# A transformer block on one core: where the output-projection weights live, when a second FFN group may open, and how the last chunk is normalized

## The chip, the cores and the metric

The kernel runs on one core of one Trainium2 chip. The metric is the device time of one execution in microseconds. Seven runs of the kernel before the change are shown, and one execution was profiled. PE is the matmul engine (TensorE), PEld its weight loads, DVE the vector engine, ACT the scalar engine, POOL GpSimd, and SP the engine that issues every DMA here.

## The reference

One pre-norm transformer block over 2048 tokens of width 1024, in bf16, with 32 heads of 32 and an FFN of width 3584:

```python
def _A_ref(x, wqkv, wo):            # attention, H = 32, Dh = 32
    ...
    scores = jnp.einsum("bhqd,bhkd->bhqk", q, k) * scale
    p = _softmax(scores, axis=-1)
    o = jnp.einsum("bhqk,bhkd->bhqd", p, v)
    return (lambda x, *d: x.transpose(*d))(o, 0, 2, 1, 3).reshape(B, S, D) @ wo

def _B_ref(x, w1, b1, w2, b2):      # FFN
    h = jnp.einsum("bsd,df->bsf", x, w1) + b1
    h = _gelu(h)                    # tanh form
    return jnp.einsum("bsf,fd->bsd", h, w2) + b2

h = x + _A_ref(_layernorm(x, axis=-1), A_wqkv, A_wo)
h2 = h + _B_ref(_layernorm(h, axis=-1), B_w1, B_b1, B_w2, B_b2)
```

## The kernel before

The tokens are cut into eight chunks of 256. Heads are handled in eight groups g of four. For each chunk c the kernel runs `attention(c)`: for each g, eight rounds over 256 keys. A round is eight score matmuls (L680), two exponentials of 128x1024 on ACT (L688), a sum of pairs PS on DVE (L693), eight matmuls with V (L698) and four with ones for the denominator (L717). At the end of a group DVE scales the result into `OT` (L726 to L734).

Beside attention runs the background work of the chunks before it. Its matmuls are all recorded by the helper `mm` (L493 in the form of four column tiles, L496 in the full form that is used after the last attention matmul). For chunk c it is, in this order: `wo(c)`, the output projection, four groups (j, t) of 8 matmuls 128x512, j being the half of the 1024 output columns and t the tile of 128 tokens; DVE adds the rows of x (L762) into `hch`; `ln2(c)`, the normalization of both tiles into `xb` (bn_stats L541, bn_aggr L543, small steps on POOL L546 to L552, normalization L555) and a transposition into `hnT` (by DMA, in the last chunk by PE and ACT, L561 and L564); `ffn1(c)`, 14 blocks of 16 matmuls with a GELU on DVE and ACT (L798 or L794, L801, L802, L804, L806) into `gT`; and `ffn2(c)`, four groups (j, t) of 29 matmuls, the first of which adds the bias, with a last step L826 and the store. ffn2(c) is interleaved with ffn1(c+1) by `PLAN`: one group, 4 blocks, one group, 5 blocks, one group, 5 blocks, one group.

Weights come in blocks of 512 KB through two rings: `w1r` with three slots and `w2r` with seven. ffn1 takes one block of w1r per block of work; ffn2 takes seven blocks of w2r for each j. wo takes four blocks: of w1r in chunks 0, 1 and 7, of w2r in chunks 2 to 6.

The order on each engine is written ahead of time by a planner in the program (`Graph.schedule`): it plays all tasks with assumed durations, and each engine's instructions are then issued in the order that it found, with semaphore waits between engines. On DVE, ACT, POOL and SP it takes the ready task with the smallest `prio`, then the oldest. On PE it takes scores first, then attention's other matmuls, then background matmuls, by the age of their group (`pick_pe`). A background group needs one of the free PSUM banks, of which attention leaves two to be shared between its own accumulator and the background. A group may open when all that it reads is done or nearly so, except what stands in its `soft` set, when each task of its `gate` has been placed, and when its loads can be issued; after attention's last matmul the oldest group may open at once. A buffer (`Buf`) is what dependencies are counted on: a task that reads a buffer waits for its writers.

After attention(7) comes the tail: half of ffn2(6), wo(7), ln2(7), the other half of ffn2(6), ffn1(7), ffn2(7). It has wider rings, `R2`, made from the memory of K and V (`slots`, names wk and wv), which is free by then.

Of the kernel before, what the change touches and what calls it, by code (L numbers as in the profile page):

```python
# [12 lines left out]
P = 128  # L13
# [299 lines left out]
def build_kernel(nc, A_x, A_wqkv, A_wo, B_w1, B_b1, B_w2, B_b2, out):  # L313
# [80 lines left out]
    RB, B_RB = sb(top, "RB", [P, NFI, 8], F32, NFI)  # L394
    pt_hi = top.cur
    NOT = 2
    OT, B_OT_ = sb(top, "OT", [P, NOT, G, 256], BF, NOT * G)
    B_OT = [B_OT_[G * s:G * s + G] for s in range(NOT)]
    NXR = 8
# [28 lines left out]
    R1 = Set()  # L428
    NW1, NW2 = 3, 7
    w1r, B_w1r = sb(ffn, "w1r", [P, NW1, 2048], BF, NW1)  # L430
    hch, B_hch_ = sb(ffn, "hch", [P, 2, 2, D], BF, 4)
    B_hch = [B_hch_[:2], B_hch_[2:]]
    x_lo = ffn.cur
    R1.x = Ring(ring(ffn, "a_x", 2, 512, BF))
    xb2 = ring(Area(x_lo), "xb2", 1, D, BF)[0]
    hnT, B_hnT = sb(ffn, "hnT", [P, 2, DC, P], BF, 2)
    R1.sq = Ring(ring(ffn, "a_sq", 2, 512, BF))
    th_lo = ffn.cur
# [94 lines left out]
    def layer_norm(tiles, prio):  # L533
        n = len(tiles)
        while cnt["ln"] % NLN + n > NLN:
            cnt["ln"] += 1
        i = cnt["ln"] % NLN
        cnt["ln"] += n
        for k, (x_ap, B_x, o_ap, B_o) in enumerate(tiles):
            for c in range(2):  # L540
                dve(lambda v, c=c, k=k, x_ap=x_ap: v.bn_stats(st_l[:, i + k, 6 * c:6 * c + 6], x_ap[:, 512 * c:512 * c + 512]),  # L541
                    0.68, reads=[B_x], writes=[B_stl[i + k]], prio=prio)
            dve(lambda v, k=k: v.bn_aggr(mv_l[:, i + k, :], st_l[:, i + k, :]), 0.2,  # L543
                reads=[B_stl[i + k]], writes=[B_mv[i + k]], prio=prio)
        sl = slice(i, i + n)
        pool(lambda g: g.tensor_copy(mvb[:, sl, :], mv_l[:, sl, :]), 0.25, reads=B_mv[sl], writes=B_mvb[sl], prio=prio)  # L546
        dve(lambda v: v.tensor_copy(mvr[:, sl, :], mvb[:, sl, 0:1]), 0.2, reads=B_mvb[sl], writes=B_mvr[sl], prio=prio)
        pool(lambda g: g.tensor_scalar(tb[:, sl, :], mvb[:, sl, 1:2], EPS_BF, None, ALU.add), 0.25,
             reads=B_mvb[sl], writes=B_tb[sl], prio=prio)
        pool(lambda g: g.tensor_tensor(denb[:, sl, 0], tb[:, sl, 0], cexp[:, 0:n], ALU.pow), 0.42 + 0.157 * n,  # L550
             reads=B_tb[sl] + [B_cexp], writes=B_denb[sl], prio=prio)
        pool(lambda g: g.tensor_tensor(rden[:, sl, 0], denb[:, sl, 0], cexp[:, 8:8 + n], ALU.pow), 0.4 + 0.157 * n,  # L552
             reads=B_denb[sl] + [B_cexp], writes=B_rden[sl], prio=prio)
        for k, (x_ap, B_x, o_ap, B_o) in enumerate(tiles):
            dve(lambda e, k=k, x_ap=x_ap, o_ap=o_ap: e.tensor_scalar(  # L555
                o_ap, x_ap, mvr[:, i + k, :], rden[:, i + k, :], ALU.subtract, ALU.mult), 0.58,
                reads=[B_x, B_mvr[i + k], B_rden[i + k]], writes=[B_o], prio=prio)

    def transposes(g, src_ap, B_src, dst_ap, B_dst, evac):
        for dc in range(DC):  # L560
# [20 lines left out]
            P * DC * (c1 - c0) * 2, writes=B_W[blk][c0 // P:c1 // P], prio=prio, after=after)  # L581

    def x_slot(tt):
        return xrb[:, tt % NXR, :], B_xrb[tt % NXR]

    def x_tile(tt, prio):
        ap, b = x_slot(tt)
        return dma(ap, x2[tt * P:(tt + 1) * P, :], P * D * 2, writes=[b], prio=prio)

    def ln_tiles(tts, prio):  # L590
        layer_norm([x_slot(tt) + (xb[:, tt % NXB, :], B_xb[tt % NXB]) for tt in tts], prio)
# [157 lines left out]
    def rows(ap, c, t, j):  # L749
        return ap[256 * c + P * t:256 * c + P * t + P, 512 * j:512 * j + 512]  # L750

    def wo(R, c, ring_):
        for j in range(2):
            ws = [w2block(ring_, A_wo[512 * q:512 * q + 512, 512 * j:512 * j + 512]) for q in range(2)]
            for t in range(2):
                x3, bx = R.x.next()
                dma(x3, rows(x2, c, t, j), P * 1024, writes=[bx], prio=1, after=lx)
                grp = group(f"wo{c}.{j}{t}")
                for g in range(G):
                    w, bw, _ = ws[g // 4]  # L760
                    mm(grp, OT[:, c % NOT, g, t * P:t * P + P], w[:, g % 4, :], g == 0, g == G - 1, [B_OT[c % NOT][g], bw])
                dve(lambda v, t=t, j=j, x3=x3, grp=grp: v.tensor_tensor(  # L762
                    hch[:, c % 2, t, 512 * j:512 * j + 512], psum[:, grp.bank, :], x3, ALU.add),
                    c_dve_ps(512), reads=[grp.buf, bx], writes=[B_hch[c % 2][t]], prio=-2)

    def ln2(c, evac):
        o, bo = xb2
        for t in range(2):
            layer_norm([(hch[:, c % 2, t, :], B_hch[c % 2][t], o, bo)], 0)
            if evac == "dma":  # L770
                dma_t(hnT[:, t, :, :], o, [bo], [B_hnT[t]], prio=-1)
            else:
                transposes(group(f"t{c}.{t}"), o, bo, hnT[:, t, :, :], B_hnT[t], evac)

    soft = {}

    def ffn1(R, c, blks, tail=False):
        for blk in blks:
            w, bw = wblock(R, B_w1[:, 256 * blk:256 * blk + 256])
            grp = group(f"f1.{c}.{blk}")  # L780
            for f in range(2):
                for dc in range(DC):
                    mm(grp, w[:, dc, f * P:f * P + P], hnT[:, :, dc, :], dc == 0, dc == DC - 1, [bw] + B_hnT,
                       cols=(256 * f, 256 * f + 256))
            (sq, b_sq), (th, b_th) = R.sq.next(), R.th.next()
            fc = 2 * blk
            xh = gT[:, c % 2, fc:fc + 2, :]
            b_xh = B_gT[c % 2][fc:fc + 2]

            def v2(ap):  # L790
                return ap.rearrange("p (f n) -> p f n", f=2)
            if tail:
                for f in range(2):
                    act(lambda a, xh=xh, f=f, fc=fc, grp=grp: a.activation(  # L794
                        xh[:, f, :], psum[:, grp.bank, 256 * f:256 * f + 256], ACT.Identity,
                        bias=b1f[:, fc + f:fc + f + 1], scale=1.0), 256, reads=[grp.buf, B_b1f], writes=[b_xh[f]], ap_bias=True)
            else:
                dve(lambda v, xh=xh, fc=fc, grp=grp: v.tensor_tensor(  # L798
                    xh, v2(psum[:, grp.bank, :]), b1f[:, fc:fc + 2].unsqueeze(2).broadcast_to((P, 2, 256)), ALU.add),
                    c_dve_ps(512), reads=[grp.buf, B_b1f], writes=b_xh, prio=-2)  # L800
            dve(lambda v, sq=sq, xh=xh: v.tensor_tensor(v2(sq), xh, xh, ALU.mult), c_dve(512, 2), reads=b_xh, writes=[b_sq], prio=1)  # L801
            dve(lambda v, sq=sq, xh=xh: v.scalar_tensor_tensor(v2(sq), v2(sq), C2, xh, ALU.add, ALU.mult), c_dve(512),  # L802
                reads=[b_sq] + b_xh, writes=[b_sq], prio=1)
            act(lambda a, th=th, sq=sq: a.activation(th, sq, ACT.Tanh, bias=0.0, scale=K2 / 2), 512,  # L804
                reads=[b_sq], writes=[b_th], prio=-1, kind="tanh")
            t = dve(lambda v, th=th, xh=xh: v.scalar_tensor_tensor(xh, v2(th), 1.0, xh, ALU.add, ALU.mult),  # L806
                    c_dve(512), reads=[b_th] + b_xh, writes=b_xh, prio=1)
            soft.setdefault(c, set()).add(t)
# [3 lines left out]
    def ffn2(R, c, j, t, tail=False):  # L812
# [3 lines left out]
        grp = group(f"f2.{c}.{j}{t}")  # L816
        grp.soft = {d for _, _, d in ws}
        grp.dmas = [d for _, _, d in ws]
        if tail:
            pass  # L820
        mm(grp, two_row[:, :], b2t[:, 512 * j:512 * j + 512], True, False, [B_two, B_b2t])
        for fc in range(FC):
            w, bw, _ = ws[fc // 4]
# [1 line left out]
        o, bo = R.os.next()  # L825
        dve(lambda v, j=j, t=t, o=o, grp=grp: v.scalar_tensor_tensor(  # L826
            o, psum[:, grp.bank, :], 0.5, hch[:, c % 2, t, 512 * j:512 * j + 512], ALU.mult, ALU.add),
            c_dve_ps(512), reads=[grp.buf, B_hch[c % 2][t]], writes=[bo], prio=-2)
        dma(rows(out2, c, t, j), o, P * 1024, reads=[bo], prio=0)

    def mixed(R, c1, c2, plan):
# [84 lines left out]
        attend(g, 0)  # L916
        attend(g, 1)

    wo(R1, 0, R1.w1)
    ln2(0, "dma")  # L920
    for k in range(4):
        late_q(2, k)
    for k in range(4):
# [8 lines left out]
            if g % 2 == 1 and c + 2 < NC:  # L932
                load_q(c + 2, g // 2)

    F2 = [(0, 0), (0, 1), (1, 0), (1, 1)]
    PLAN = [F2[0], 4, F2[1], 5, F2[2], 5, F2[3]]
    ffn1(R1, 0, range(FC // 2))
    for c in range(2, NC):
        wo(R1, c - 1, R1.w1 if c == 2 else R1.w2)
        ln2(c - 1, "dma")  # L940
        mixed(R1, c - 1, c - 2, PLAN)
        attention(c)
    L = NC - 1
    TA = 2
    tail = Area(pt_lo, pt_hi)
    R2 = Set()
    R2.sq = Ring(ring(tail, "b_sq", 4, 512, BF))
    R2.th = Ring(ring(tail, "b_th", 4, 512, F32))
    R2.os = Ring(ring(tail, "b_os", 2, 512, BF))
    slots = []  # L950
    for k in range(7):
        for lo, nm in ((kt_lo, "wk"), (v_lo, "wv")):
            slots += ring(Area(lo + 4096 * k), f"{nm}{k}", 1, 2048, BF)
    for jt in F2[:TA]:
        ffn2(R1, L - 1, *jt)
    wo(R1, L, R1.w1)
    ln2(L, "act")
    for jt in F2[TA:]:
        ffn2(R1, L - 1, *jt)
    k = R1.w1.k % NW1  # L960
    R2.w1 = Ring(slots[:11] + R1.w1.slots[k:] + R1.w1.slots[:k])
    R2.w2 = Ring(slots[11:] + R1.w2.slots)
    ffn1(R2, L, range(FC // 2), True)
    for jt in F2:
        ffn2(R2, L, *jt, True)
# [161 lines left out]
```

## Time and profile before

| | |
|---|---|
| median of 7 runs | 1144.76 us (1141.82 to 1148.82) |
| the profiled execution | 1144.76 us, span 1143.0 us |
| busy PE / ACT / DVE | 1070.1 / 1037.8 / 823.5 us |
| L688, the exponentials | 1024 instructions, 967.0 us busy |
| L493, ffn1's matmuls | 6272 instructions, 221.2 us busy |
| loads w2r<-wo / w1r<-wo | 20 / 12 issues of 512 KB |
| mean granted TensorE clock | 0.990 |

A row of the profile gives a line of the kernel, the engine, the operation, the tile written and the tiles read, the number of instructions, and the busy time. The four column tiles of one background matmul count as four instructions, and overlap. A number in square brackets in a timeline is the time that the engine stood idle before this row, with what released it. The time of one execution is 1.8 us longer than the profile's span, which runs from the first instruction to the last.

### The profile page before, as it was taken

The numbers are of one execution on the slowest core, as the hardware profiler recorded it, in microseconds if no ns is written. First come the engines' busy times: TensorE is split into PE (matmuls) and PEld (weight loads), VectorE is DVE, ScalarE is ACT, GpSimd is POOL, SyncE is SP. The second block draws the span as 40 slices with busy tenths as digits, with TensorE's granted clock in tenths as the row PEclk, the third lists the DMA queues.
The fourth block names the chain that finished last, engine by engine and source line by source line (L and its number), as shares of the span: only waits on it lengthen the run. The fifth ranks groups of instructions, "written<-read, shape, count | busy, mean of one in ns | idle before, by whom it ended". The sixth has DMA issues, their size and how long they took to land.

```text
span 1143.0 us, 53683 instructions
## 1 busy us (share of the span) xinstructions
PE 1070.1 (94%) x24933; PEld 608.8 (53%) x24939; DVE 823.5 (72%) x1552; ACT 1037.8 (91%) x1185; POOL 43.8 (4%) x108
## 2 busy tenths in 40 slices
PE   8979999999999989999999999999998989899998
PEld 6636464655445535654654555455545634555484
DVE  7345666666768977886897878777877866777572
ACT  4869999999999999999999999999999999999460
POOL 3200000000100010001000100100010001000000
PEclk9989999999999989999999999999999989999999
DMA  8860100001435536476637574764657456868742
GB/s 208 179 152 5 47 4 3 3 22 49 118 99 162 154 100 208 130 220 186 199 110 234 152 213 132 209 205 131 208 154 232 116 175 180 270 187 261 241 134 92
DMA packets 265137, 168.09 MB, mean 147 GB/s; under 512 B 56017, under 2 KB 262865, under 8 KB 264914
## 3 DMA queue, kind: packets, MB, share of 16 engines
q1 hardware_dynamic: 264914, 164.67, 49.3%
q8 instruction: 195, 3.19, 1.1%
q14 instruction: 28, 0.23, 0.1%
HBM read 151.00 MB, written 6.29 MB: 138 GB/s over the span
## 4 chain that ended last, share of the span: by engine, by line
PE 53%; ACT 34%; DVE 5%; DMA 3%; SPq 2%; issue 2%; POOL 1%; DVEq 0%; POOLq 0%
ACT PT L688 32%; PE ps L493 30%; PE ps L680 8%; PE ps L496 5%; PE ps L698 5%; PE ps L717 3%; ACT a_th L804 2%; SPq L514 2%; DVE gT L798 1%; PE ps L850 1%; DMA hnT<-xb 1%; DVE PS L693 1%; DMA q_scratch<-stg 1%; DMA b1b<-in_B_b_dram 1%; DVE gT L806 1%
## 5 line engine op out<-in xcount | busy, mean ns | idle before, releaser
L688 ACT ACTIVATE PT<-ps 128x1024 bf16<-128x1024 f32 x1024 | 967.0, 1050 | 35.8 <-PE ps L680 32.7
L693 DVE TENSOR_TENSOR PS<-PT 128x1024 bf16<-128x1024 bf16 x496 | 329.1, 683 | 87.7 <-ACT PT L688 49.8
L493 PE MATMUL ps<-hnT,w1r 128*32 128x256 bf16 x6272 | 221.2, 274 | 17.5 <-issue 6.8
L680 PE MATMUL ps<-QT,KT 32*128 32x256 bf16 x4096 | 206.1, 275 | 16.5 <-ACT PT L688 12.7
L698 PE MATMUL ps<-PT,V 128*32 128x256 bf16 x4096 | 188.6, 275 | 14.0 <-ACT PT L688 10.1
L493 PE MATMUL ps<-w2r,gT 128*32 128x512 bf16 x2936 | 196.8, 382 | 0.6 <-issue 0.6
L493 PEld LDWEIGHTS ps<-hnT,w1r 128*32 128x32 bf16 x6272 | 155.4, 96 | 60.3 <-issue 44.8
L680 PEld LDWEIGHTS ps<-QT,KT 32*128 32x128 bf16 x4096 | 61.1, 92 | 170.9 <-ACT PT L688 124.0
L717 PE MATMUL ps<-PS,ones 128*32 128x256 bf16 x1984 | 143.5, 277 | 2.7 <-DVE PS L693 1.3
L493 PE MATMUL ps<-xnT,Wall 128*32 128x512 bf16 (+1 forms) x2144 | 129.9, 357 | 7.6 <-DVE QT L574 6.5
L698 PEld LDWEIGHTS ps<-PT,V 128*32 128x32 bf16 x4096 | 99.1, 96 | 65.5 <-ACT PT L688 30.9
L493 PEld LDWEIGHTS ps<-w2r,gT 128*32 128x32 bf16 x2936 | 69.8, 96 | 66.4 <-issue 23.7
L798 DVE TENSOR_TENSOR gT<-ps,b1f 128x512 bf16<-128x512 f32 x98 | 67.3, 687 | 34.3 <-PE ps L493 33.2
L717 PEld LDWEIGHTS ps<-PS,ones 128*32 128x32 bf16 x1984 | 53.0, 96 | 43.5 <-DVE PS L693 28.4
L493 PEld LDWEIGHTS ps<-xnT,Wall 128*32 128x32 bf16 x2144 | 51.0, 97 | 46.0 <-issue 14.5
L806 DVE SCALAR_TENSOR_TENSOR gT<-a_th,gT 128x512 bf16<-128x512 f32 x98 | 67.2, 685 | 11.5 <-ACT a_th L804 11.2
L802 DVE SCALAR_TENSOR_TENSOR a_sq<-a_sq,gT 128x512 bf16<-128x512 bf16 x98 | 66.7, 687 | 1.4
L804 ACT ACTIVATE a_th<-a_sq 128x512 f32<-128x512 bf16 x98 | 64.2, 656 | 2.3 <-DMA q_scratch<-stg 1.5
L493 PE MATMUL ps<-Wall,xnT 128*32 128x256 bf16 x1536 | 51.3, 273 | 1.6 <-DVE KT L574 1.0
L493 PE MATMUL ps<-w2r,OT 128*32 128x512 bf16 x640 | 46.1, 391 | 1.1 <-DVE hch L762 0.5
L546 POOL CAST mvb<-mv 128x2 bf16<-128x2 f32 (+1 forms) x24 | 4.9, 203 | 1036.2 <-DVE mv L543 1031.8
L726 DVE STREAM_TRANSPOSE DT<-ps 128x256 f32<-128x256 f32 x64 | 28.6, 447 | 21.0 <-PE ps L717 20.8
(76 smaller groups left out, 687.5 us busy)
## 6 DMA issues: line engine op xcount, KB each, us to landing
w2r<-in_B_w_dram SPq DMA_DIRECT2D x106, 512.0 KB, 6.2
w1r<-in_B_w_dram SPq DMA_DIRECT2D x101, 512.0 KB, 4.2
w2r<-in_A_wo_dram SPq DMA_DIRECT2D x20, 512.0 KB, 5.6
w1r<-in_A_wo_dram SPq DMA_DIRECT2D x12, 512.0 KB, 3.8
wv<-in_B_w_dram SPq DMA_DIRECT2D x9, 512.0 KB, 5.3
xrb<-in_A_x_dram SPq DMA_DIRECT2D x16, 256.0 KB, 3.9
Wall<-in_A_wqkv_dram SPq DMA_DIRECT2D x16, 256.0 KB, 5.1
a_x<-in_A_x_dram SPq DMA_DIRECT2D x32, 128.0 KB, 2.7
```

The source lines that it names most:

```text
L493: fns.append(lambda p, j=j: p.matmul(dst(32 * j, 32 * j + 32), lhsT[:, 32 * j:32 * j + 32], rhs, start=start, stop=stop, tile_position=(0, ...
L496: t.alt = [lambda p: p.matmul(dst(0, P), lhsT, rhs, start=start, stop=stop, skip_group_check=True)]
L680: fns.append(lambda p, i=i, hh=hh, r0=r0: p.matmul(psum[:, 2 * us[hh // 2] + hh % 2, 256 * i:256 * i + 256], KT[r0:r0 + 32, g, 256 * r + P ...
L688: act(lambda a, u=u, q=q: a.activation(PT[:, s, 2 * q:2 * q + 2, :], psum[:, 2 * u:2 * u + 2, :], ACT.Exp, bias=0.0, scale=SCALE), 1024, r ...
L693: dve(lambda v: v.tensor_tensor(PS[:, z, :, :], PT[:, s, :, 0:256], PT[:, s, :, 256:512], ALU.add), c_dve(1024, 2), reads=B_PT[s], writes= ...
L698: fns.append(lambda p, i=i, hh=hh: p.matmul(psum[32 * hh:32 * hh + 32, self.bank, 0:256], V[:, g, 2 * r + i, 32 * hh:32 * hh + 32], PT[:, ...
L717: fns.append(lambda p, i=i, hh=hh, src=src: p.matmul(psum[32 * hh:32 * hh + 32, self.bank, 256:512], ones32[:, :], src[:, hh, :], start=False,
L726: dve(lambda v: v.transpose(DT[:, f, :], psum[:, self.bank, 256:512]), c_dve_ps(256), reads=[self.buf], writes=[B_DT[f]], prio=-1)
L798: dve(lambda v, xh=xh, fc=fc, grp=grp: v.tensor_tensor(xh, v2(psum[:, grp.bank, :]), b1f[:, fc:fc + 2].unsqueeze(2).broadcast_to((P, 2, 25 ...
L802: dve(lambda v, sq=sq, xh=xh: v.scalar_tensor_tensor(v2(sq), v2(sq), C2, xh, ALU.add, ALU.mult), c_dve(512), reads=[b_sq] + b_xh, writes=[ ...
L804: act(lambda a, th=th, sq=sq: a.activation(th, sq, ACT.Tanh, bias=0.0, scale=K2 / 2), 512, reads=[b_sq], writes=[b_th], prio=-1, kind="tanh")
L806: t = dve(lambda v, th=th, xh=xh: v.scalar_tensor_tensor(xh, v2(th), 1.0, xh, ALU.add, ALU.mult), c_dve(512), reads=[b_th] + b_xh, writes= ...
```

## The change

1. `wo` always takes its four blocks from w1r, so that w2r serves ffn2 alone. In the last chunk all wo blocks come from the wide ring R2.w1.
2. An ffn2 group no longer waits with its opening for the last steps of the GELUs (`grp.soft |= soft[c]`); it may open once the last ffn1 block's first step out of PSUM has been placed (`grp.gate`). Each of its matmuls still waits for its own gT.
3. `hch` is tracked in eight buffers, by chunk, tile and half, where it was four; bn_stats of a half and ffn2's last step wait for that half alone.
4. The steps of ln2 have priority -2 where they had 0.
5. In the last chunk wo runs tile by tile, with the tile's normalization after its two groups, two buffers for the normalized tile (in K's memory) where there was one, and four buffers for the rows of x (in QT) where there were two. All four ffn2(6) groups now stand after it in the order of groups. R2.w1 keeps 14 slots, four of which serve wo first; R2.w2 has 9 where it had 10.

```diff
-    hch, B_hch_ = sb(ffn, "hch", [P, 2, 2, D], BF, 4)
-    B_hch = [B_hch_[:2], B_hch_[2:]]
+    hch, B_hch_ = sb(ffn, "hch", [P, 2, 2, D], BF, 8)
+    B_hch = [B_hch_[:4], B_hch_[4:]]
...
+    LN2_PRIO = -2
...
-                    0.68, reads=[B_x], writes=[B_stl[i + k]], prio=prio)
+                    0.68, reads=[B_x[c % len(B_x)]], writes=[B_stl[i + k]], prio=prio)
...
+    def wo_w(R, j):
+        return [w2block(R.w1, A_wo[512 * q:512 * q + 512, 512 * j:512 * j + 512]) for q in range(2)]
+
+    def wo_group(R, c, j, t, ws):
+        x3, bx = R.x.next()
+        dma(x3, rows(x2, c, t, j), P * 1024, writes=bx, prio=1, after=lx)
+        grp = group(f"wo{c}.{j}{t}")
+        for g in range(G):
+            w, bw, _ = ws[g // 4]
+            mm(grp, OT[:, c % NOT, g, t * P:t * P + P], w[:, g % 4, :], g == 0, g == G - 1, [B_OT[c % NOT][g], bw])
+        dve(lambda v: v.tensor_tensor(hch[:, c % 2, t, 512 * j:512 * j + 512], psum[:, grp.bank, :], x3, ALU.add),
+            c_dve_ps(512), reads=[grp.buf] + bx, writes=[B_hch[c % 2][2 * t + j]], prio=-2)
+
+    def wo(R, c):
         for j in range(2):
+            ws = wo_w(R, j)
             for t in range(2):
+                wo_group(R, c, j, t, ws)
+
+    def ln2_tile(R, c, t, evac):
+        o, bo = R.xb.next()
+        layer_norm([(hch[:, c % 2, t, :], B_hch[c % 2][2 * t:2 * t + 2], o, bo)], LN2_PRIO)
...
-                    act(lambda a, xh=xh, f=f, fc=fc, grp=grp: a.activation(
+                    gate[c] = act(lambda a, xh=xh, f=f, fc=fc, grp=grp: a.activation(
...
-                dve(lambda v, xh=xh, fc=fc, grp=grp: v.tensor_tensor(
+                gate[c] = dve(lambda v, xh=xh, fc=fc, grp=grp: v.tensor_tensor(
...
-        if tail:
-            pass
+        grp.soft |= soft[c]
+        grp.gate = [gate[c]]
...
-            c_dve_ps(512), reads=[grp.buf, B_hch[c % 2][t]], writes=[bo], prio=-2)
+            c_dve_ps(512), reads=[grp.buf, B_hch[c % 2][2 * t + j]], writes=[bo], prio=-2)
...
-        wo(R1, c - 1, R1.w1 if c == 2 else R1.w2)
-        ln2(c - 1, "dma")
+        wo(R1, c - 1)
+        ln2(R1, c - 1, "dma")
...
-    TA = 2
...
+    R2.x = Ring([(QT[:, k:k + 2, :].rearrange("p s t -> p (s t)"), B_QT[k:k + 2]) for k in range(8, 16, 2)])
...
-    for jt in F2[:TA]:
-        ffn2(R1, L - 1, *jt)
-    wo(R1, L, R1.w1)
-    ln2(L, "act")
-    for jt in F2[TA:]:
+    R2.xb = Ring(ring(Area(kt_lo), "xbl", 2, D, BF))
+    k = R1.w1.k % NW1
+    R2.w1 = Ring(slots[1:12] + R1.w1.slots[k:] + R1.w1.slots[:k])
+    R2.w2 = Ring(slots[12:] + R1.w2.slots)
+    ws = [wo_w(R2, j) for j in range(2)]
+    for t in range(2):
+        for j in range(2):
+            wo_group(R2, L, j, t, ws[j])
+        ln2_tile(R2, L, t, "act")
+    for jt in F2:
         ffn2(R1, L - 1, *jt)
-    k = R1.w1.k % NW1
-    R2.w1 = Ring(slots[:11] + R1.w1.slots[k:] + R1.w1.slots[:k])
-    R2.w2 = Ring(slots[11:] + R1.w2.slots)
```

More of the change, by code (lines that the diff above doesn't have):

```diff
@@ L396, in build_kernel @@
     NOT = 2
+    F2 = [(0, 0), (0, 1), (1, 0), (1, 1)]
     OT, B_OT_ = sb(top, "OT", [P, NOT, G, 256], BF, NOT * G)
@@ L430, in build_kernel @@
     w1r, B_w1r = sb(ffn, "w1r", [P, NW1, 2048], BF, NW1)
-    hch, B_hch_ = sb(ffn, "hch", [P, 2, 2, D], BF, 4)
-    B_hch = [B_hch_[:2], B_hch_[2:]]
+    hch, B_hch_ = sb(ffn, "hch", [P, 2, 2, D], BF, 8)
+    B_hch = [B_hch_[:4], B_hch_[4:]]
     x_lo = ffn.cur
-    R1.x = Ring(ring(ffn, "a_x", 2, 512, BF))
-    xb2 = ring(Area(x_lo), "xb2", 1, D, BF)[0]
+    R1.x = Ring([(h, [b]) for h, b in ring(ffn, "a_x", 2, 512, BF)])
+    R1.xb = Ring(ring(Area(x_lo), "xb2", 1, D, BF))
+    LN2_PRIO = -2
     hnT, B_hnT = sb(ffn, "hnT", [P, 2, DC, P], BF, 2)
@@ L556, in layer_norm @@
                 o_ap, x_ap, mvr[:, i + k, :], rden[:, i + k, :], ALU.subtract, ALU.mult), 0.58,
-                reads=[B_x, B_mvr[i + k], B_rden[i + k]], writes=[B_o], prio=prio)
+                reads=B_x + [B_mvr[i + k], B_rden[i + k]], writes=[B_o], prio=prio)
     def transposes(g, src_ap, B_src, dst_ap, B_dst, evac):
@@ L583, in x_slot @@
     def x_slot(tt):
-        return xrb[:, tt % NXR, :], B_xrb[tt % NXR]
+        return xrb[:, tt % NXR, :], [B_xrb[tt % NXR]]
     def x_tile(tt, prio):
         ap, b = x_slot(tt)
-        return dma(ap, x2[tt * P:(tt + 1) * P, :], P * D * 2, writes=[b], prio=prio)
+        return dma(ap, x2[tt * P:(tt + 1) * P, :], P * D * 2, writes=b, prio=prio)
     def ln_tiles(tts, prio):
@@ L750, in rows @@
         return ap[256 * c + P * t:256 * c + P * t + P, 512 * j:512 * j + 512]
-    def wo(R, c, ring_):
+    def wo_w(R, j):
[9 more added lines that the diff above has]
+            c_dve_ps(512), reads=[grp.buf] + bx, writes=[B_hch[c % 2][2 * t + j]], prio=-2)
@@ L753, in wo @@
+    def wo(R, c):
         for j in range(2):
-            ws = [w2block(ring_, A_wo[512 * q:512 * q + 512, 512 * j:512 * j + 512]) for q in range(2)]
+            ws = wo_w(R, j)
             for t in range(2):
[L756 to L764, printed above, removed]
@@ L766, in ln2 @@
-    def ln2(c, evac):
-        o, bo = xb2
-        for t in range(2):
[L769 to L775, printed above, removed]
+                wo_group(R, c, j, t, ws)
+    def ln2_tile(R, c, t, evac):
+        o, bo = R.xb.next()
+        layer_norm([(hch[:, c % 2, t, :], B_hch[c % 2][2 * t:2 * t + 2], o, bo)], LN2_PRIO)
+        if evac == "dma":
+            dma_t(hnT[:, t, :, :], o, [bo], [B_hnT[t]], prio=-1)
+        else:
+            transposes(group(f"t{c}.{t}"), o, bo, hnT[:, t, :, :], B_hnT[t], evac)
@@ L777, in ffn1, with ln2 @@
+    def ln2(R, c, evac):
+        for t in range(2):
+            ln2_tile(R, c, t, evac)
+    soft, gate = {}, {}
     def ffn1(R, c, blks, tail=False):
@@ L917, in build_kernel @@
         attend(g, 1)
-    wo(R1, 0, R1.w1)
-    ln2(0, "dma")
+    wo(R1, 0)
+    ln2(R1, 0, "dma")
     for k in range(4):
@@ L933, in attention @@
                 load_q(c + 2, g // 2)
-    F2 = [(0, 0), (0, 1), (1, 0), (1, 1)]
     PLAN = [F2[0], 4, F2[1], 5, F2[2], 5, F2[3]]
```

## The prediction

> **What bounds the kernel now.** First the page's busy shares and chain, then the chain's shares against stage windows, then the list of waits by engine, then the background matmuls (`mm`, L493/L496) in the timeline, last the DMA queue's timeline.
>
> ```profile
> PE 1070.1 (94%) x24933; PEld 608.8 (53%) x24939; DVE 823.5 (72%) x1552; ACT 1037.8 (91%) x1185; POOL 43.8 (4%) x108
> PE 53%; ACT 34%; DVE 5%; DMA 3%; SPq 2%; issue 2%; POOL 1%; DVEq 0%; POOLq 0%
> 80.00:1069.00 989.00, 931.15 (x23492) 522.80 (x23484) 745.64 (x1390) 964.92 (x1081) 23.79 (x56) 0.99 0.48 144
> ACT PT L688 <- PE ps L680: 18.7, 26, 2.4
> ```
>
> The third line is a window over the attention stage (columns: stretch, length, busy PE, PEld, DVE, ACT, POOL, clock, DMA share, GB/s), the fourth ACT's waits in it. ACT is busy 965 of 989 us and waits 18.7 us for score matmuls: the exponentials set this stage's length. From 1071.6 to 1140 us PE alone sets it: there it waits 0.3 us in all. So only two things count: ACT's idle time before 1069, and how much matmul work is left for after it.
>
> The background matmuls are not continuous. Two stretches of the PE timeline hold attention alone:
>
> ```profile
> 405.79 1.26 PE L493 MATMUL ps<-w1r,OT 128*32 128x512 bf16 x20
> ...
> 409.26 0.40 PE L680 MATMUL ps<-QT,KT 32*128 32x256 bf16 x8 [0.40 <-ACT PT L688]
> ...
> 417.13 0.62 PE L493 MATMUL ps<-b2t,two_row 128*32 128x512 bf16 x4
> ```
>
> ```profile
> 928.30 0.83 PE L493 MATMUL ps<-w2r,gT 128*32 128x512 bf16 x12
> ...
> 934.10 0.40 PE L698 MATMUL ps<-PT,V 128*32 128x256 bf16 x8 [0.52 <-ACT PT L688]
> ...
> 939.28 1.47 PE L493 MATMUL ps<-w2r,OT 128*32 128x512 bf16 x12
> ```
>
> Background work ends at 407.6 and resumes at 417.1 (9.5 us); again 929.1 to 939.3 (10.2 us). What each waited for is in the DVE and the DMA-issue timelines:
>
> ```profile
> 403.57 0.69 DVE L806 SCALAR_TENSOR_TENSOR gT<-a_th,gT 128x512 bf16<-128x512 f32 x1
> ...
> 416.26 0.69 DVE L806 SCALAR_TENSOR_TENSOR gT<-a_th,gT 128x512 bf16<-128x512 f32 x1
> ```
>
> ```profile
> 922.66 3.40 SPq L514 DMA_DIRECT2D w2r<-in_A_wo_dram  x4
> 927.00 3.68 SPq L514 DMA_DIRECT2D w2r<-in_B_w_dram  x3
> ```
>
> The first ended when the last GELU of chunk 0 (416.26 + 0.69) released ffn2(0). In the second, ffn2(5) has all its GELUs, but four of the ring's seven slots hold output-projection weights for wo(6), whose input is complete only at 939; only three ffn2 blocks could be issued, the others came at 946 and 953. After both, the clock and ACT suffer:
>
> ```profile
> 417.00:424.00 7.00, 7.00 (x116) 3.05 (x116) 2.08 (x3) 5.16 (x7) 0.00 (x0) 0.71 0.26 70
> 939.00:944.00 5.00, 5.00 (x72) 1.82 (x64) 1.86 (x4) 3.17 (x4) 0.00 (x0) 0.57 0.01 3
> 421.12 12.26 ACT L688 ACTIVATE PT<-ps 128x1024 bf16<-128x1024 f32 x13 [1.84 <-PE ps L680]
> 943.27 29.85 ACT L688 ACTIVATE PT<-ps 128x1024 bf16<-128x1024 f32 x32 [1.83 <-PE ps L680]
> ```
>
> Windows, then ACT's timeline: granted clock 0.71 and 0.57, score matmuls 0.61 us instead of 0.40, and each time ACT idles 1.8 us.
>
> **The change part by part.**
>
> *Sums.* The profiled execution took 1144.76 us, span 1143.0; 1144.76 is also the median of the seven runs, so terms go against it directly.
>
> *Opening ffn2 early.* Nothing is added to any engine; groups take a bank sooner. At 407.6 ffn2(0) can open, with the ready blocks first and the last at 416: the 9.5 us are filled. In the last chunk the rule gives nothing: its first ffn2 group is first in line, opened at 1114.96, and the last GELU ran at 1118.48 without a PE gap. The added wait: PE is in order, so behind an early ffn2 matmul that waits for a late GELU stand score matmuls. Bounds: 0 (blocks are consumed in the order in which GELUs finish) to 1.8 us of ACT idle per case (the rows above); I take 0.
>
> *Ring.* The 20 loads of wo blocks that used w2r (wo(2) to wo(6), 512 KB each) go to w1r: bytes and issues are equal. ffn2(5)(0,0) then has its seven loads from 922.7 on. Neighbouring rows: the DMA stretch 924 to 933 moved up to 386 GB/s, busy stages 275; seven blocks (3.67 MB) need 9.5 to 13.3 us, ending at 932 to 936, so I count 8 of the 10.2 us as filled. wo(c)'s fourth block must now wait for wo(c)(0,1) to free a slot: see the second rival. I take 0, since the boundary at 394 to 407.6 already ran so: 13.7 us for 128 matmuls, against 12.6 to 15.7 at boundaries with w2r.
>
> *ACT.* With background work kept up, the two clock drops and their 1.84 + 1.83 go: **-3.7 us**. The other 15 us of ACT's idle time I leave, ±3 for a newly ordered program.
>
> *The clock.* Trace: drops began 3.2 and 7.4 us after background work stopped, though PE was still busy 6.3 of 9 us (window 408 to 417), and ended 4.0 us after it resumed. [...]
>
> *Tail, what is left over.* At 1071.6 there remain 51 ffn2(6) matmuls (22 + 29) of 0.216 us (1.03 us for four pipelined, 0.865 start to start): 11.0 us. With wo(7), 32 x 0.216 = 6.9, and transposes (0.6), they are the 18.6 us from 1071.62 to ffn1's start at 1090.25. The 17.5 us filled earlier hold 53 matmuls at attention's pace (29 in 9.5 us: 0.33 each), so nearly all 51 are done before. What is late next is the normalization chain. With tiles in order, early x rows in QT, and statistics by half, it runs after the last wo matmul: 0.2 + add 0.69 (L762) + one statistic 0.69 (L541) + aggregate and POOL 2.09 (1084.65 to 1086.74) + normalize until transposes 0.91 + transposes 0.65 + ACT copy 1.02 (L564) + 0.1 = 6.4 us. Before, its x row landed only at 1081.42 and the two tiles shared one buffer, 9.6 us, hidden by ffn2. So ffn1 starts 6.9 + 6.4 = 13.3 us after 1071.6: -5.3. The cover is gone then: PE idles up to 5 us, and the clock may fall. By the rows above (4.0 us at half speed after a resumption) that costs 0 to 2.0; I take 0.8: -5.3 + 0.8 = **-4.5 us.**
>
> *Tail, w2 slots.* ffn2(7)'s ring falls from 10 to 9: five blocks instead of four are loaded while (0,1) runs. Four were issued at 1122.33 to 1124.86 and landed 4.1 to 7.0 us later, about 1.8 apart; the fifth is needed 11.7 us after (0,1) starts and lands at 12.5. Bounds 0 to 1.8: **+0.8 us.** ffn1's last four blocks reuse wo's slots 17 us ahead of need: 0.
>
> *LN priority.* The normalization's DVE steps (2 x 0.69 + 0.2 + 0.14 + 0.55 = 2.3 us a tile) now pass the pair sums PS and, by age, evacuations; behind them queue denominators, PV and then scores. Twelve tiles lie in attention; the only near row is PE waiting 1.3 us in five cases for PS. Bounds -1 (LN earlier) to +4: **+1.0 us.** The split hch buffers add no instruction.
>
> Sum: -3.7 - 4.5 + 0.8 + 1.0 = -6.4 us: **1138.4 us.** Seven runs spread 1141.8 to 1148.8, so about 0.3% (3.4 us) can be told from no change.
>
> **The rivals.**
>
> *The hole moves (25%).* Background work is a fixed sum: ffn2 run ahead leaves the end of attention(7) empty, wo(7) starts at half clock (4.0 us: +2.0) and ffn1 too (+2.0 instead of 0.8). For: 53 against 51 matmuls is a close balance. Against: ffn2(6)'s second half needs its ring reloaded and so is spread late. Then -1.84 (first drop only) - 5.3 + 2.0 + 2.0 + 0.8 + 1.0 = -1.3: 1143.4 us, within 0.3%.
>
> *The fourth wo block (17%).* In a ring of three, wo(c)'s fourth block is issued after (0,1). In the tail of before it went out at 1074.23 and wo resumed at 1077.92, 3.7 us; in mid-kernel it stands behind seven ffn2 loads. If ffn2(c-1) is used up or unloaded, each of five boundaries starves, and break-even is 17.5 / 5 = 3.5 us each. At 5 us: 7.5 us net, 23 matmuls more in the tail, +4.9; no clock gain; + 0.8 + 1.0: 1151.5 us, slower. Against: the boundary at 394, and that a ready ffn2 group may pass a wo group that is not.
>
> **How the numbers follow.** Forecast 58%, the hole 25%, the fourth block 17%. The forecast's own range is 1133 (-5.3 in the tail, no LN or ring cost, -3) to 1141.4 (all terms as taken, +3). The full range reaches 1150: it takes in the hole and leaves out most of the last rival. Faster by over 0.3%: 57%; within: 25%; slower: 18%.
>
> **What would show it.** Right: PE background matmuls between 408 and 417 and near 930; no clock below 1 after 80 us; ACT's waits for scores near 15 us; wo(7) to ffn1 about 13 to 14 us; ffn1-to-end unchanged within 1 us. Wrong: a gap in wo(c) between its third and fourth block with no ffn2 inside, a new clock drop near 1065, or ACT waits above 20 us, at DVE PS or gT.

## The result and the profile after

The changed kernel is slower: 1154.63 us median of 13 runs, against 1145.73 us for 34 runs of the kernel before; ratio 1.0076, 95% interval 1.0058 to 1.0093, or 8.7 us of 1145. The forecast was 1138.4. All ratios below are to runs of the kernel before on the same chip, since its median was 1144.97 to 1148.37 us from chip to chip.

The page's busy line and chain of the changed kernel, and ACT's waits in its attention stage (80 to 1078 us; sum, times, longest):

```profile
PE 1068.8 (93%) x25079; PEld 611.4 (53%) x25083; DVE 823.2 (72%) x1552; ACT 1039.6 (90%) x1185; POOL 48.8 (4%) x108
PE 55%; ACT 24%; DVE 9%; DMA 5%; issue 2%; SPq 2%; POOL 1%; POOLq 0%; DVEq 0%
ACT PT L690 <- PE ps L682: 24.9, 31, 2.8
```

The work is the same (DVE and ACT run 1552 and 1185 instructions in both; busy PE, DVE and ACT agree within 0.2%; PE's counts are those of the records, of which some are missing). In the chain DVE's share has grown from 5 to 9% and DMA's from 3 to 5%. ACT waits 24.9 us for scores where it waited 18.7. By stages, counted from the two traces:

| us | before | after |
|---|---|---|
| 41st exponential to the end of the last | 991.4 | 999.9 |
| wo(7)'s first matmul to ffn1(7)'s | 18.6 | 14.3 |
| ffn1(7) to ffn2(7) | 24.7 | 26.7 |
| ffn2(7)'s first matmul to its last, start to start | 24.6 | 24.6 |
| ffn2(6) matmuls on record between wo(7)'s start and ffn1(7) | 49 | 3 |

So the tail gained 2.3 us and attention lost 8.5. The two holes of before are filled, and a new one stands at 972. Windows of the changed kernel over the two old places, the new one and the 5 us behind it (columns as in the prediction):

```profile
408.00:417.00 9.00, 8.69 (x192) 4.17 (x192) 8.20 (x16) 8.96 (x11) 2.07 (x3) 1.00 0.08 25
929.00:939.00 10.00, 10.00 (x216) 4.68 (x218) 6.51 (x13) 9.95 (x12) 0.00 (x0) 1.00 0.57 178
974.00:985.00 11.00, 7.98 (x148) 2.66 (x143) 8.02 (x18) 11.00 (x13) 3.13 (x4) 0.74 1.02 249
985.00:990.00 5.00, 5.00 (x96) 2.89 (x89) 0.93 (x2) 3.29 (x4) 0.00 (x0) 0.56 0.00 0
```

The background matmuls around it, from PE's timeline:

```profile
971.60 0.60 PE L495 MATMUL ps<-w2r,gT 128*32 128x512 bf16 x8
985.18 1.28 PE L495 MATMUL ps<-hnT,w1r 128*32 128x256 bf16 x20
```

All of ffn2(5) had been used up before wo(6) was done, and ln2(6) ran with nothing to put beside it: 13 us, and the granted clock at 0.50 again (979.2 to 989.4 us). But ACT waited only about 1.8 us behind this hole, as behind each of the old ones. The 6 us that ACT lost lie elsewhere. At 849 us it made its longest wait; in order of cause, from the timelines of SP, DVE, PE and ACT:

```profile
837.74 3.00 SPq L520 DMA_TRANSPOSE hnT<-xb  x1
840.78 2.65 SPq L516 DMA_DIRECT2D w2r<-in_B_w_dram  x4
846.21 1.80 SPq L520 DMA_TRANSPOSE hnT<-xb  x1
```

```profile
845.64 0.55 DVE L557 TENSOR_SCALAR xb<-hch,mvr,rden 128x1024 bf16<-128x1024 bf16 x1 [3.15 <-DMA hnT<-xb]
846.10 2.49 DVE L695 TENSOR_TENSOR PS<-PT 128x1024 bf16<-128x1024 bf16 x4
```

```profile
846.84 0.29 PE L719 MATMUL ps<-PS,ones 128*32 128x256 bf16 x4 [2.58 <-DVE PS L695]
849.09 1.02 ACT L690 ACTIVATE PT<-ps 128x1024 bf16<-128x1024 f32 x1 [2.85 <-PE ps L682]
```

The first tile's transposition was issued at 837.74 with three weight loads of 512 KB still in flight (two of w1r for ffn1, in the slots that wo had just left, and one of w2r), and four more of w2r followed it. It landed 7.8 us later. The second tile's normalization (L557) needs the one xb buffer which that transposition reads, and it stands first in DVE's order: DVE idled 3.15 us, with four pair sums queued behind it. PE, in order too, stood at the ones-matmul that needs the first of them, the scores behind that came late, and ACT ran dry. The same chain appears at 731 us (1.71 us of ACT).

How long the transpositions took over the whole program (tile hnT on SP: issue to landing, min/median/max), with PE's and DVE's waits behind them from 80 to 1080 us (sum, times, longest). Before:

```profile
DMA to landing us min/median/max: 2.7/3.4/4.5
PE ps L717 <- DVE PS L693: 1.3, 5, 0.5
PE ps L493 <- DMA hnT<-xb: 1.5, 1, 1.5
DVE xb L555 <- DMA hnT<-xb: 5.2, 3, 2.9
```

After (13 of the 14 transpositions have a landing on record):

```profile
DMA to landing us min/median/max: 2.7/5.9/8.5
PE ps L719 <- DVE PS L695: 5.8, 7, 2.6
PE ps L495 <- DMA hnT<-xb: 2.4, 3, 0.9
DVE xb L557 <- DMA hnT<-xb: 9.2, 5, 3.2
```

Before, the first transposition of a pair was issued with one or two loads of 512 KB in flight (once with three), and the second always with none; after, twelve of the fourteen had two to four (counted from the loads' issue and landing times).

Seven of ACT's waits for scores in the changed kernel's attention stage stand directly behind a late transposition (at 435, 529, 630, 635, 731, 734 and 849 us, together 8.0 us); before, one did (1.6 us at 746). These 6.4 us are about what ACT's waits for scores grew by, 18.7 to 24.9.

### The profile page after: what moved, and what is told of

The parts are those of the page before. It is cut to its first block, busy times and chain, and to the rows that moved or that the text cites. A ratio compares the mean times of both kernels' runs of the same rounds, so it can differ in the third digit from the quotient of the medians.

```text
span 1149.1 us, 53988 instructions
## 1 busy us (share of the span) xinstructions
PE 1068.8 (93%) x25079; PEld 611.4 (53%) x25083; DVE 823.2 (72%) x1552; ACT 1039.6 (90%) x1185; POOL 48.8 (4%) x108
## 4 chain that ended last, share of the span: by engine, by line
PE 55%; ACT 24%; DVE 9%; DMA 5%; issue 2%; SPq 2%; POOL 1%; POOLq 0%; DVEq 0%
PE ps L495 32%; ACT PT L690 23%; PE ps L682 8%; PE ps L498 6%; PE ps L700 5%; DMA hnT<-xb 4%; PE ps L719 3%; DVE PS L695 3%; DVE gT L808 2%; SPq L516 2%; ACT a_th L814 1%; DVE gT L816 1%; PE ps L860 1%; DMA xnT<-xb 1%; DVE a_sq L812 1%
## 5 line engine op out<-in xcount | busy, mean ns | idle before, releaser
L495 PE MATMUL ps<-hnT,w1r 128*32 128x256 bf16 x6272 | 218.8, 275 | 22.7 <-issue 9.2
L495 PE MATMUL ps<-w2r,gT 128*32 128x512 bf16 x3124 | 215.9, 381 | 1.1 <-DVE gT L816 1.1
L495 PEld LDWEIGHTS ps<-w2r,gT 128*32 128x32 bf16 x3124 | 74.2, 96 | 66.0 <-issue 24.5
L495 PE MATMUL ps<-w1r,OT 128*32 128x512 bf16 x896 | 59.2, 381 | 1.1 <-DVE QT L576 0.5
L495 PEld LDWEIGHTS ps<-Wall,xnT 128*32 128x32 bf16 x1536 | 38.0, 96 | 9.8 <-issue 6.5
```

The source lines that it names most:

```text
L495: fns.append(lambda p, j=j: p.matmul(dst(32 * j, 32 * j + 32), lhsT[:, 32 * j:32 * j + 32], rhs, start=start, stop=stop, tile_position=(0, ...
```

## The experiments

The theories, as the expectations name them. A: the ring of three delays wo's fourth block, wo splits, and ffn1 runs in long stretches. B: the normalization's priority makes DVE wait in order. C: early opening breaks the order. D: the ring brings ffn2's loads into the queue when ln2's transpositions run, so that they land later than the planner assumed, and DVE, PE and ACT wait one behind the other.

### One part undone, one part alone

The ring undone:

```diff
-            ws = wo_w(R, j)
+            ws = wo_w(R.w2 if c >= 2 else R.w1, j)
...
```

> The changed kernel with one part undone: in chunks 2 to 6 the four output-projection blocks come from the seven-slot ring again. Theory A (the three-slot ring delays wo's fourth block, wo splits, ffn2 groups are used up as filler and ffn1 runs in long stretches in which PE's instruction supply and DVE fall behind): the cost is gone, ACT's idle time in attention is back near 18 us, and the tail's gain of about 2 us remains: 1141 to 1144 us. Theory B (normalization at priority -2 blocks DVE behind a transposition): 1150 us or more, since the priority is kept. Theory C (groups opened early hold a bank and break the order): 1150 us or more, since early opening is kept.

Measured: 1148.72 against 1148.37 us, ratio 1.0004 (0.9982 to 1.0025). Without the shared ring the loss is gone, though the priority and the early opening are kept, so these two by themselves do not make it. The tail's gain that the expectation counted on is not there: 51 matmuls of ffn2(6) are left for the tail, and wo(7) to ffn1(7) takes 19.2 us. DVE waits 13.5 us for xb here, longer than in the changed kernel, but PE only 2.3 us for PS: DVE's wait costs where it reaches PE.

The ring alone, on the kernel before:

```diff
-        wo(R1, c - 1, R1.w1 if c == 2 else R1.w2)
+        wo(R1, c - 1, R1.w1)
```

> The kernel before with one part of the change: every output projection takes its blocks from the three-slot ring. Theory A: slower than before by 4 to 8 us (1150 to 1154), with the splits of wo and runs of 9 to 14 ffn1 blocks. Theories B and C: within 3 us of before, since neither the priority nor the opening rule is changed.

Measured: ratio 1.0012 (0.9993 to 1.0031). wo splits as theory A says, and ffn1 runs in stretches of up to 14 blocks, but this alone costs at most 0.3%. The signs of theory D are there in full: transpositions land in 5.0 us in the median, PE waits for them and for PS in the profiled run for 11.6 us (8.2 in the changed kernel), and 6.9 us of ACT's waits stand behind them:

```profile
PE ps L717 <- DVE PS L693: 6.4, 9, 2.1
PE ps L493 <- DMA hnT<-xb: 5.2, 2, 2.6
```

So the waits come with the ring alone, and yet no loss stands out of the noise. The run-ahead gives something back (33 matmuls of ffn2(6) are left, and wo(7) to ffn1(7) takes 17.2 us), and this execution, of 1152.82 us, is slower than the median of its kernel, 1148.97. Whether these two explain it is not shown.

The written order held (a gate on the ffn1 blocks that stand before each ffn2 group):

```diff
-        grp.gate = [gate[c]]
+        grp.gate = [gate[c], *before]
...
-                ffn2(R, c2, *p)
+                ffn2(R, c2, *p, before=[gate[c1]] if blk else [])
```

> The changed kernel, with the second to fourth ffn2 group of each chunk also gated on the ffn1 blocks that stand before them in the written order, so that ffn1 no longer runs in stretches of 9 to 14 blocks; the ring, the early opening against the GELUs and the priority are kept. Theory A in the form that the long ffn1 runs are the cost: 1142 to 1147 us and ACT's waits with the cause 'issue' fall from 9 us to under 4. If the split of wo or the DVE wait for the transposition is the cost: 1150 us or more.

Measured: 1164.72 against 1148.37 us, ratio 1.0150 (1.0114 to 1.0187). The long ffn1 stretches are not the cost: without them it is worse, and the fastest version below has stretches of up to 14 blocks too. The ffn2 groups that are held back no longer stand beside ln2: PE's wait for hnT grows from 2.4 to 7.5 us, and the mean granted clock of the profiled run is 0.979, against 0.990 in the changed kernel's. This ends theory A in that form.

The tail alone (the changed kernel with ring, priority and opening rule as before):

```diff
-    LN2_PRIO = -2
+    LN2_PRIO = 0
...
-        grp.soft |= soft[c]
-        grp.gate = [gate[c]]
...
-            ws = wo_w(R, j)
+            ws = wo_w(R.w2 if c >= 2 else R.w1, j)
```

> The kernel before with the fifth part alone (last chunk tile by tile, its wider buffers, ffn2(6) behind wo(7) in order) and the finer hch buffers; ring, opening rule and priority as before. All theories: attention as before, the tail shorter by 2 to 4 us: 1142 to 1144 us. If it is not faster, the tail's gain that the two traces show (18.6 to 14.3 us from wo(7) to ffn1(7), less 2 us for a slow clock) is given back elsewhere.

Measured: ratio 1.0012 (0.9991 to 1.0033): no gain, and the expectation was wrong. 51 ffn2(6) matmuls are left, and PE has no gap from wo(7) to ffn1(7) in either kernel; a shorter normalization chain is worth nothing while that filler covers it. The run-ahead alone does not give the whole gain either: with the old order and 33 matmuls left (the ring alone) this stretch takes 17.2 us, with the new order and 29 left (no early opening, below) 14.4. It takes both, less filler and the shorter chain.

In this run's profile attention takes 997.7 us, 6.3 more than in that of the kernel before, though the ratio is 1.0012. Stage times of single executions, in a newly planned order and on another chip, can differ by that much without the ring, the priority or the opening.

The priority back at 0 (`LN2_PRIO = 0`, all else as changed):

> The changed kernel with the normalization's priority back at 0; ring, early opening and tail kept. Theory B (at priority -2 the normalization's last step stands first in DVE's queue and waits there for the transposition by DMA that still reads the one xb buffer, with the pair sums behind it): 1146 to 1150 us on this chip (before 1146 to 1148), the waits of the ones-matmuls for PS fall from 5.8 to under 2 us. Theory D (what costs is that the ring brings seven ffn2 loads into the queue while the normalization's transpositions run, so that both DVE and PE wait for them, whatever the priority): still 1153 us or more. Theory C (early opening): still 1153 us or more.

Measured: 1152.77 against 1147.63 us, ratio 1.0034 (1.0019 to 1.0050). The time lies between what B and what D expected: the priority is part of the loss, not the whole of it. PE's wait for PS falls from 5.8 to 3.3 us.

No early opening (the two lines of `grp.soft` and `grp.gate` out, all else as changed):

> The changed kernel without the early opening of ffn2 groups; ring, priority and tail kept. Theory C: 1146 to 1150 us. Theories B and D: still 1153 us or more. From the ring alone (same as before within 0.3%) I hold it possible that the ring and the early opening cost only together, which this run would show as a time near before's.

Measured: 1150.24 against 1147.63 us, ratio 1.0031 (1.0006 to 1.0057), between the expectations again. Here too the loss shrinks and does not go; the intervals of these two runs overlap with each other and lie below the changed kernel's.

Early opening alone, on the kernel before:

> The kernel before with the early opening of ffn2 groups alone. The prediction's term: the hole at 408 to 417 us is filled and its clock drop gone (1.8 us of ACT), nothing else changes much: 1143 to 1147 us. Theory C: 1150 us or more.

Measured: 1143.91 against 1147.63 us, ratio 0.9963 (0.9945 to 0.9980). Alone it gains, 4.2 us by the ratio: the hole at 408 is filled and its clock drop gone, as the prediction had it (score matmuls take 0.40 us from 400 to 419 us, and not 0.61; that the gain is more than the drop's 1.8 us is not explained by a run). Theory C falls as far as the opening alone goes; beside the ring the opening is part of the loss, as the run without it shows.

Each of these edits makes the planner lay the whole order anew, so a difference of some 0.3% can also come from the order. How the loss divides among the parts is not shown.

### The planner's number for a transposition

One number in the planner, in all places; no instruction is added:

```diff
-prio, nbytes=P * D * 2)
+prio, nbytes=P * D * 2 * 4)
```

> The changed kernel, with one number of the planner changed: it counts a transposition by DMA as four times its bytes (3.6 us of queue instead of 0.9), so that it puts the steps which wait for one later in DVE's and PE's order. No instruction is added. Theory D (and B): the waits behind transpositions (ones-matmuls for PS, ffn1 for hnT) fall under 2 us together and the time falls to 1146 to 1150 us. If the cost lies elsewhere (instruction supply in long ffn1 stretches, clock): 1153 us or more.

Measured: 1145.10 against 1147.63 us, ratio 0.9970 (0.9953 to 0.9987). PE no longer waits for hnT, and for PS 2.3 us. From the 41st exponential on attention takes 986.1 us, 13.8 less than in the changed kernel. The lead before it grew, since the first layer norm's transpositions were planned later as well: the 41st exponential starts at 89.8 us, in the other runs at 75 to 82.

The same number in ln2 alone:

```diff
-            dma_t(hnT[:, t, :, :], o, [bo], [B_hnT[t]], prio=-1)
+            dma_t(hnT[:, t, :, :], o, [bo], [B_hnT[t]], prio=-1, k=4)
```

> The changed kernel with the planner's number for a transposition by DMA four times as large in ln2 alone (the first layer norm keeps its order). Theory D: the changed kernel's loss is its late transpositions, and what the run with the number changed everywhere lost in the lead (exponential number 40 at 89.8 us instead of 79) comes back: 1134 to 1140 us where before is 1145 to 1148; waits of the ones-matmuls for PS and of ffn1 for hnT under 3 us together. If that run's gain came from another order by chance: 1143 us or more.

Measured: 1134.45 against 1144.97 us, ratio 0.9896 (0.9871 to 0.9920). This version beats both kernels. Its transpositions still land late; only DVE, PE and ACT hardly stand still for them any more (views as above, the last line over 80 to 1062 us):

```profile
DMA to landing us min/median/max: 2.7/5.3/7.0
PE ps L719 <- DVE PS L695: 2.7, 7, 0.9
DVE xb L557 <- DMA hnT<-xb: 0.4, 1, 0.4
ACT PT L690 <- PE ps L682: 12.5, 18, 2.2
```

None of ACT's waits stands behind a transposition here. Attention is 13.1 us shorter than in the changed kernel; 8.0 of these were the waits behind transpositions. The clock drop at 979 is gone too (granted 1.00 from 80 to 1060 us); the rest comes with the new order, and no run divides it.

The control, the same edit on the kernel before:

> The control: the kernel before with the same number changed in ln2 alone. Before, a transposition lands in 3.4 us on the average (after: 5.6), its waits cost PE 1.5 us and ACT 1.6. Theory D: a gain of 1 to 4 us, a third or less of what the changed kernel gets from the same edit (12 us). If the edit helps this kernel as much, the optimism is no part of what the change did.

Measured: ratio 1.0007 (0.9979 to 1.0034): no gain; the expected 1 to 4 us lie within the interval only at their lower end. The same edit that takes 1.8% from the changed kernel takes nothing from the kernel before, which had 1.6 us of ACT's waits behind transpositions, so it is no general improvement of the order.

The same edit with the ring undone:

> The changed kernel with the wo blocks of chunks 2 to 6 on the seven-slot ring and the planner's number changed in ln2: what the shared ring is worth once the transpositions' waits are planned for. The prediction's term (run-ahead at 930 us, a shorter tail since little of ffn2(6) is left): 3 to 6 us slower than the run with the shared ring and the same number. If the ring brings nothing: equal within 2 us.

Measured: ratio 0.9975 (0.9956 to 0.9995), on the chip of the run with 0.9896. The shared ring is then worth 0.8%, some 9 us, more than the 3 to 6 expected: in the profiled runs ffn2(6) leaves 12 matmuls for the tail with the ring and 58 without, wo(7) to ffn1(7) takes 13.7 against 20.7 us, and attention 986.8 against 992.9.

### The suspected cost put onto the kernel before

Two copies of 512 KB within device memory ahead of each transposition, counted by the planner as no bytes; nothing reads what they write:

```diff
+                for q in range(2):
+                    dma(spare[512 * q:512 * q + 512, :], A_wo[512 * q:512 * q + 512, 0:512], 0, prio=-2, after=bo.w)
                 dma_t(hnT[:, t, :, :], o, [bo], [B_hnT[t]], prio=-1)
```

> The kernel before with two copies of 512 KB within device memory issued right ahead of every ln2 transposition, which the planner counts as no bytes; nothing reads them. It puts onto before what theory D says the ring did: loads in flight when a transposition is issued. Theory D: transpositions land in 6 us or more instead of 3.4, waits for hnT and for PS rise by 5 us or more, and the time rises by 4 to 12 us. If the time stays within 2 us, late transpositions are not what costs.

Measured: 1182.76 against 1144.97 us, ratio 1.0323 (1.0297 to 1.0349), more than expected. The lines that carry it (tile hnT on SP, then the waits of DVE and PE from 80 to 1080 us and of ACT to 1069; attention ends at 1107):

```profile
DMA to landing us min/median/max: 5.6/7.1/8.0
DVE xb L556 <- DMA hnT<-xb: 33.2, 7, 7.9
PE ps L718 <- DVE PS L694: 14.5, 13, 5.0
ACT PT L689 <- PE ps L681: 54.4, 36, 6.3
```

Late transpositions that the order does not expect are enough to slow this kernel by the same chain: xb, PS, scores, exponentials. Some 31 us of ACT's waits stand directly behind a transposition; for weight loads, which the copies could have delayed as well, PE waits 2.1 us in all (0.5 before). The copies move more than the ring does, so the run shows the mechanism and not the size.

## Why the prediction was wrong

*The step that failed* is the ring's term, "I take 0", and with it the +1.0 us for the normalization's priority. For the ring the prediction counted bytes, issues and wo's fourth block, and asked whether the seven early loads help ffn2; it did not ask what else stands in that queue. Two to four loads of 512 KB, of w1r as well as of w2r, are in flight when most of ln2's transpositions are issued, and the transpositions' time to landing went from 3.4 to 5.9 us in the median. The second tile's normalization waits behind them for the one xb buffer, the pair sums stand behind it in DVE's order, and PE and ACT behind those: 8.0 us of ACT's waits, where it was 1.6. The row was to be had before: DVE already waited 5.2 us in three cases for xb behind hnT, and PE once 1.5 us for hnT. The priority step looked only at the 1.3 us that PE waited for PS (and counted twelve tiles; the transpositions are fourteen).

With the ring undone the ratio goes from 1.0076 to 1.0004, so in this company its term is about +8 us and not 0; with the priority undone it goes to 1.0034, about 5 us where +1.0 stood; with the early opening undone to 1.0031, also about 5 us, where its cost was taken as 0. These do not add up: ring and tail alone cost nothing that can be measured, and early opening alone gains 0.4%. The same program with the transpositions planned for is 1.8% faster (0.9896 against 1.0076, some 20 us, of which 8.0 were the waits behind transpositions); without the ring the same edit is worth 0.3%. Of the signs of being wrong that the prediction named, ACT's waits above 20 us, at DVE's PS, is the one that came.

*Opening ffn2 early*: the gain was right. The hole at 408 is filled (8.69 of 9 us busy), and alone it gave 4.2 us. The cost of 0 holds alone, and not beside the ring.

*ACT, -3.7 us*: both old clock drops are gone as said (granted 1.00 from 81.5 to 979.2 us), and one came back at 979. With the transpositions planned for, attention takes 986.8 us where it took 991.4, so -4.6 (1.6 of it the one wait behind a transposition that the kernel before had); as the change stands, +8.5.

*Tail, -4.5 us*: from wo(7) to ffn1(7) -4.4 measured, forecast -5.3; ffn1 +2.0 from the clock (granted 0.50 from 1091.8 to 1098.7 us), which was taken as 0.8 and bounded by 2.0. PE's timeline shows the uncovered chain and a slow start:

```profile
1092.27 1.01 PE L563 MATMUL ps<-ident,xbl 128*128 128x128 bf16 x8 [2.74 <-DVE xbl L557]
1094.39 1.89 PE L498 MATMUL ps<-hnT,wv 128*128 128x256 bf16 x8 [1.12 <-ACT hnT L566]
```

Eight matmuls take 1.89 us there; later in the tail sixteen take 1.91. *Tail, w2 slots*: +0.8 forecast, 0 measured.

*The rivals.* "The hole moves" was right that a hole appears and that ffn1(7) starts slowly (+2.0), and wrong on the place: the hole stands at 972 to 985, in ln2(6), and not at the end of attention(7), where ffn2(6) runs on to 1079. It gave no change, since it priced no new wait. "The fourth wo block" had the sign (1151.5), and wo did split, but its mechanism was wrong: the ready ffn2 groups filled the gap, as its "against" said.

Where PE's waits with the cause "issue" come from (up to 2.3 us each in the changed kernel), behind which ACT waits too, is open. They make up 7 to 17 us in every profiled run, also in those without long stretches, and no run here was made to tell their cause.

## What to carry to other kernels

When loads are freed to go earlier, look at what shares their queue at that moment, and at who waits for it in order: a transposition that took 2.7 us at best took 7.8 behind three loads, and one in-order engine after another stood behind it. Where an order is written ahead of time, a duration that is too short can be harmless, as it was in the kernel before, until a change puts the wait under load; giving the planner a larger number for the contended step turned a loss of 0.8% into a gain of 1.0% with no change in the work. And a shorter chain was worth nothing while filler covered it (ratio 1.0012 with 51 matmuls of filler left): first count the filler.

## What the runs showed of the hardware that was not expected

A DMA transposition of 256 KB landed in 2.7 us at best, with no 512 KB load in flight at its issue (in 4.5 us at most, in the kernel before), and in up to 8.5 us with four; its issue alone held SP for 1.2 to 2.4 us before and 1.2 to 3.4 us after. Every DMA here is issued from SP, so the runs show only that a transposition lands later beside loads of the same issuer, with these numbers.

The granted clock fell to 0.50 at 979.2 us, for 10.2 us. In the 6.7 us from 972.3 to 979, after background work had stopped, PE was busy for 4.65 us (69%), in short pieces: the clock fell under a PE that was not idle.
